# A gated mix of attention and an MLP: where the statistics' transposes, the first block's norming and the raw MLP weights stand in the opening stage

## The chip, the cores and the metric

The kernel runs on one core of one Trainium2 chip. The metric is the device time of one execution, in microseconds (us). Lower is better. TensorE (PE) multiplies matrices, VectorE (DVE) and ScalarE (ACT) empty its accumulation banks (PSUM) and do elementwise work, GpSimd (POOL) does elementwise work on on-chip tiles, and SyncE (SP) issues nearly all the DMA transfers. Each engine works through its own instructions in the order in which the program lists them.

## The reference

With S = 2048 tokens, D = 576 channels, 32 heads of 18 and F = 4608 hidden units, for one input `x`:

```
g = sigmoid((x * gate_w).sum(-1, keepdims=True))
q, k, v = split of x @ wqkv into 32 heads
a = softmax(q k^T / sqrt(18)) v, heads joined, @ wo
y = (x - mean) / sqrt(var + 1e-5)
b = gelu(y @ w1 + b1) @ w2 + b2
out = g * a + (1 - g) * b
```

Everything is float32. The kernel splits operands of the large products into a high and a low part of a faster 32-bit format and adds three products (high by high, low by high, high by low).

## The kernel before

**Two stages.** The opening stage goes through the tokens in four blocks of 512 (`tb` 0 to 3) and computes Q, K, V and the normed input of the MLP, which it parks in DRAM (`qk_scr`, `v_scr`, `y_scr`). It takes about the first 250 us. Then a loop of 512 steps weaves attention (scores, exponentials, products with V) and the MLP's matmuls, one instruction list for the whole rest. All order is written by hand: there is no scheduler behind it. What stands in a program list first runs first on its engine.

**A block** has 17 steps `g`: nine Q/K groups (`qk_group`, 14 matmuls of 512 columns, L879 to L882) and eight V groups (`v_group`, 14 matmuls of 288 columns, L900 to L903). Each group fills one of four PSUM banks (`ps_a`), and ACT (L885, L907) and DVE (L886, L911) empty it. From the group's values the high part `hh` and low part `hl` are made, and SP stores them (L888, L889, L914). Between groups stand these helpers, at steps that a table gives:

- `norm(tb, 0)` and `norm(tb, 1)`: DVE takes mean and variance of 256 tokens each (L847, L848); stage 1 ends with a square root on ACT (L854) and a chain of small DVE operations up to a reciprocal (L853 to L860). `norm(tb, 2)` and `norm(tb, 3)` form the gate's logits (L865). For block 0 alone they also norm `x` in place (L868).
- `stat_rows(tb)`: DVE copies means and reciprocals into a tile `stp` (L826, L827), PE transposes it (L829), ACT copies it out (L830) and SP stores it (L831). `load_wide(tb)` reads it back spread over all partitions into `wide` (L835). `wide` lies in the tile `qa`.
- `x_chunk(tb, c)`, c = 0 to 4: PE transposes 128 channels of `x` (L758), DVE subtracts the mean (L773, for blocks 1 to 3), ACT and DVE make high and low part (L775, L776), POOL multiplies by the reciprocal (L783). `y_parts`, `lag` steps later, makes the normed chunk's `hh` and `hl` (L798, L799), and SP stores them (L790, L792).
- `y_chunk(0, c)`: the same for block 0, from the `x` that `norm(0, 2)` and `norm(0, 3)` have normed in place: transposes (L758), L806, L807, store.
- `split_w` halves the QKV weights, seven portions during block 0 (L752, L753); `load_x(tb)` loads the next tokens into one of two buffers `x`.
- Rounds of scores (`next_round`): four matmuls (L227) and four maxima on DVE (L229), from block 1 on. They use four more PSUM banks.

`BLOCK[tb]` holds the steps of block `tb` at which the helpers for block `tb + 1` stand: `stats` (stages 0 and 1 at this step and the next), `rows`, `wide`, `gate` (stages 2 and 3), `x` (the first of five chunks), `lag`, `load`. `N_AT` does it for block 0's own norming. Within one step the group comes first, then the norming of block 0, then the helpers of the next block, then rounds.

**The MLP's generator** `mlp()` is stepped by hand in the opening stage: its first step issues the loads of raw weights (`load_w1`, L371; `load_w2`, L377) into the two buffers `x`, its second sets up the loads of the normed high part of block 0 (`high`, copied by ACT at L631). `defer(n, fn)` runs `fn` at the n-th `run_due` from now; the opening stage calls `run_due` as `SLOTS` tells.

Of the kernel before, what the change touches and what calls it, by code (L numbers as in the profile page):

```python
# [8 lines left out]
F32 = mybir.dt.float32  # L9
# [7 lines left out]
P = 128  # L17
# [7 lines left out]
TB = 512  # L25
# [29 lines left out]
          lambda g: 2 * (g in (4, 5, 6, 7, 8, 10, 12, 14))]  # L55
SLOTS = [lambda g: 0, lambda g: 0, lambda g: int(g >= 4), lambda g: 1 if g < 9 else 2]
SKIP = 0
N_AT = 5
BLOCK = [dict(stats=3, rows=5, wide=7, gate=9, x=12, lag=3, load=13),
         dict(stats=0, rows=2, wide=3, gate=3, x=5, lag=2, load=0),  # L60
         dict(stats=0, rows=2, wide=3, gate=3, x=5, lag=2)]
W_AT = {0: 1, 1: 2, 2: 3, 4: 4, 6: 5, 7: 6}
W_CUT = (0, 128, 416, 704, 992, 2 * D, 3 * D - 288, 3 * D)
NSTEP = 512
# [4 lines left out]
def gated_mix_kernel(ctx: ExitStack, tc: tile.TileContext, x, wqkv, wo, w1, b1, w2, b2, gate_w, out):  # L69
    nc = tc.nc  # L70
    x = x[0]
# [20 lines left out]
    gate = const.tile([P, NT], F32, name="gate")  # L92
# [8 lines left out]
    pp = ctx.enter_context(tc.tile_pool(name="pp", bufs=2))  # L101
# [41 lines left out]
    def defer(n, fn):  # L143
        later.append((slot[0] + n, fn))
# [191 lines left out]
    def mlp():  # L336
# [26 lines left out]
        def load_w1(q):  # L363

            if (1, q) in LOADED or q >= NQ0:
                return
            LOADED[1, q] = slot[0] + LAND
            fc = chunk(q)[2]
            for h in range(2):
                src = w1[:, (fc + h) * P:(fc + h + 1) * P]  # L370
                nc.sync.dma_start(raw1(q)[64 * h:64 * h + 64], src.rearrange("(c p) n -> p c n", p=64))  # L371

        def load_w2(c):
            if (2, c) in LOADED or c >= NFC:
                return
            LOADED[2, c] = slot[0] + LAND
            nc.sync.dma_start(raw2(c), w2[c * P:(c + 1) * P, :])  # L377
# [241 lines left out]
                HT.pop((i, j))  # L619
                W2.pop((i * (G // 2) + j // 2, j % 2))  # L620

        for q in range(2):
            load_w1(q)
            for c in range(2 * q, 2 * q + 2):
                load_w2(c)
        yield 1
        Y[0] = big_tile()

        def high(c):
            dma_r(nc.sync, Y[0][0:64, c:c + 3, :], y_scr[0, 0, c:c + 3].rearrange("c p n -> p c n"))  # L630
            defer(6, lambda: nc.scalar.activation(Y[0][64:128, c:c + 3, :], Y[0][0:64, c:c + 3, :], AF.Copy))  # L631
        for c in range(0, 9, 3):
            defer(1 + 2 * c // 3, lambda c=c: high(c))
        yield 1
        prep(0)
        prep_w2(0)
# [16 lines left out]
        for i in range(n + 1):  # L653
            q = 2 * i
# [14 lines left out]
    stream = [mlp()]  # L669
# [36 lines left out]
    with ExitStack() as a:  # L706
# [127 lines left out]
            rows = bcast_rows(st_scr[tb], 8 * P)  # L834
            nc.sync.dma_start(wide, rows.rearrange("p (a n) -> p a n", a=2))  # L835

        rstds = {}

        def norm(tb, stage):

            xv = x_view(tb)
            ts_ = slice(4 * tb, 4 * tb + 4)
            if stage < 2:
                for t in (2 * stage, 2 * stage + 1):
                    st6 = sm.tile([P, 2, nc.vector.BN_STATS_DIM], F32, name="st6")
                    for n in range(2):
                        nc.vector.bn_stats(st6[:, n, :], xv[:, t, n * ND:(n + 1) * ND])  # L847
                    nc.vector.bn_aggr(stats[:, tb * 4 + t, :], st6)  # L848
            if stage == 1:
                rstd = rstds[tb] = sm.tile([P, 4], F32, name="rstd")  # L850
                sd = sm.tile([P, 4], F32, name="sd")
                var = sm.tile([P, 4], F32, name="var")
                nc.vector.tensor_scalar(var, stats[:, ts_, 1], LN_EPS, None, op0=ALU.add)  # L853
                nc.scalar.activation(sd, var, AF.Sqrt)  # L854

                nc.vector.reciprocal(rstd, sd)
                nc.vector.tensor_mul(rstd, rstd, var)
                nc.vector.tensor_add(sd, sd, rstd)
                nc.vector.tensor_scalar(sd, sd, 0.5, None, op0=ALU.mult)
                nc.vector.reciprocal(rstd, sd)  # L860
            if stage >= 2:
                junk = pp.tile([P, 2, 2, TB], F32, name="p").rearrange("p a b c -> p (a b c)")
                for t in (2 * stage - 4, 2 * stage - 3):
                    tt = 4 * tb + t
                    nc.vector.scalar_tensor_tensor(junk[:, :D], xv[:, t, 0:D], 1.0, gwb, op0=ALU.mult, op1=ALU.mult,  # L865
                                                   accum_out=glog[:, tt:tt + 1])
                    if tb == 0:
                        nc.vector.tensor_scalar(xv[:, t, :], xv[:, t, :], stats[:, tt, 0:1], rstds[tb][:, t:t + 1],  # L868
                                                op0=ALU.subtract, op1=ALU.mult)
# [66 lines left out]
        for tb in range(NB):  # L936
            work = [(qk_group, (tb, mt)) for mt in (range(9) if tb < 2 else (4, 0, 1, 2, 3, 5, 6, 7, 8))] + [(v_group, (tb, t, n)) for t in range(4) for n in range(2)]
            for g, (fn, args) in enumerate(work):
                if tb == 0:
                    if g in W_AT:  # L940
                        n = W_AT[g]
                        split_w(n, nc.gpsimd if 2 < n < 6 else nc.vector)
                        if n + 2 < 7:
                            load_w(n + 2)
                    if g == 10:
                        nc.sync.dma_start(b2b, bcast_rows(b2, D))
                        nc.sync.dma_start(b1r, b1.rearrange("(c p) -> c p", p=P))
                if tb == NB - 1 and g == 16:
                    args += (lambda: next(stream[0]),)
                fn(*args)  # L950
                next_turn()
                if tb == 0:
                    if 0 <= g - N_AT < 4:
                        norm(0, g - N_AT)
                    if 0 <= g - 8 < 5:
                        y_chunk(0, g - 8)
                if tb + 1 < NB:
                    at = BLOCK[tb]
                    if g == at.get("load"):
                        load_x(tb + 2)  # L960
                    if g in (at["stats"], at["stats"] + 1):
                        norm(tb + 1, g - at["stats"])
                    if g == at["rows"]:
                        stat_rows(tb + 1)
                    if g == at["wide"]:
                        load_wide(tb + 1)
                    if g in (at["gate"], at["gate"] + 1):
                        norm(tb + 1, g - at["gate"] + 2)
                    c = g - at["x"]
                    if 0 <= c < 5:  # L970
                        x_chunk(tb + 1, c)
                        after(at["lag"], lambda tb=tb, c=c: y_parts(tb + 1, c))
                if tb == 2 and g == 11:
                    next(stream[0])
                if tb == NB - 1:
                    if g == 1:
                        load_k(0, 3 * TB, S)
                    if g == 2:
                        load_q(1)
                        next(stream[0])  # L980
                    if g == 9:
                        qkstack.close()
                        wp1 = mstack.enter_context(tc.tile_pool(name="m_w1", bufs=3))
                        wp2 = mstack.enter_context(tc.tile_pool(name="m_w2", bufs=4))
                        next(stream[0])

                        nc.scalar.activation(gate, glog, AF.Exp, scale=-1.0)
                    if g == 14:
                        nc.vector.tensor_scalar(gate, gate, 1.0, None, op0=ALU.add)
                        nc.vector.reciprocal(gate, gate)  # L990
                        nc.vector.tensor_scalar(gate1, gate, -1.0, 1.0, op0=ALU.mult, op1=ALU.add)
                    if g == 7:
                        ps = psum(ps_a)
                        nc.tensor.transpose(ps[:, :NFC], b1r, ident[:NFC, :NFC])
                        nc.vector.tensor_copy(b1t, ps[:, :NFC])
                if tb == 1 and g == 5:
                    load_q(0)
                    load_k(0, 0, TB)
                if tb == 1 and g == 9:
                    load_k(0, TB, 2 * TB)  # L1000
                if tb == 2 and g == 10:
                    for c0, c1 in ((0, 3), (3, 5)):
                        dma_r(nc.sync, low[0:64, c0:c1], y_scr[0, 1, c0:c1].rearrange("c p n -> p c n"))
                        defer(6, lambda c0=c0, c1=c1: nc.scalar.activation(low[64:128, c0:c1], low[0:64, c0:c1], AF.Copy))
                if tb == 2 and g == 4:
                    load_k(0, 2 * TB, 3 * TB)
                for _ in range(ROUNDS[tb](g)):
                    next_round()
                for _ in range(SLOTS[tb](g)):
                    run_due()  # L1010
# [306 lines left out]
```

## Time and profile before

| | |
|---|---|
| median of 3 runs | 2264.46 us (2262.61 to 2265.9) |
| the profiled execution | 2265.41 us, its span 2263.6 us, mean granted clock 0.995 |
| busy over the span | PE 98%, DVE 73%, ACT 63%, POOL 44% |
| bytes moved by DMA | 329.23 MB, 145 GB/s |

A row of the timeline gives start, length, engine, line, operation, output<-input, count, and in brackets how long the engine stood idle before it and what ended that. Rows of one kind that follow each other are merged (x12), and a row's length overlaps the next one's start a little, since matmuls are pipelined. A row of the windows gives for each engine the busy time in that stretch, then the granted clock of PE as a share of full speed, the DMA engines' busy share and the GB/s. A row of the waits gives the total, the number of waits and the longest.

### The profile page before, as it was taken

The page shows a single profiled execution, that of the slowest core. Times are in us where ns is not written, and L with a number is a line of the kernel's source. Part 1 is how long each engine was busy: PE and PEld are TensorE (multiplying, and loading weights), DVE is VectorE, ACT ScalarE, POOL GpSimd, SP SyncE. Part 2 cuts the span into 40 slices and gives each one's busy share as a digit, 9 for nine tenths or more (in the row PEclk, how much of TensorE's full clock was granted, in tenths as well). Part 3 has the DMA queues.
Part 4 walks back from the last instruction along what each step waited for, and adds up shares of the span by engine and source line. Part 5 has one row for each costly group of instructions (what it writes and reads, how often), then busy time and mean ns, then how long its engine had stood idle before and what let it go on. Part 6 is the DMA issues. An engine that isn't in the chain of part 4 may idle for free.

```text
span 2263.6 us, 51585 instructions
## 1 busy us (share of the span) xinstructions
PE 2224.4 (98%) x20528; PEld 1585.9 (70%) x20528; DVE 1646.2 (73%) x2886; ACT 1428.2 (63%) x2653; POOL 1002.5 (44%) x1001
## 2 busy tenths in 40 slices
PE   7999999999999999999999999999999999999999
PEld 5877766667667676676776767667676767767668
DVE  5565677777777777777777777777777777777734
ACT  3322676777776666666666666666665666666772
POOL 3311556666665444444452444444444444444710
PEclk9999999999999999999999999999999999999999
DMA  7747644445456533333254523243354323332264
GB/s 232 259 163 230 224 154 160 147 152 163 140 191 175 160 102 116 101 114 128 98 159 149 169 99 118 101 136 105 116 170 150 106 97 113 110 129 95 101 219 165
DMA packets 164104, 329.23 MB, mean 145 GB/s; under 512 B 56814, under 2 KB 84074, under 8 KB 153134
## 3 DMA queue, kind: packets, MB, share of 16 engines
q1 hardware_dynamic: 161766, 322.19, 43.8%
q8 instruction: 162, 2.65, 0.5%
q10 hardware_dynamic: 1968, 3.70, 0.4%
q14 instruction: 80, 0.66, 0.1%
q0 software_dynamic: 128, 0.03, 0.0%
HBM read 233.47 MB, written 96.17 MB: 146 GB/s over the span
## 4 chain that ended last, share of the span: by engine, by line
PE 87%; DVE 2%; ACT 1%; DMA 1%; issue 1%; POOL 1%; SPq 0%; ACTq 0%; POOLq 0%
PE ps L285 20%; PE ps L572 19%; PE ps L484 19%; PE ps L267 13%; PE ps L227 10%; PE ps L1202 3%; PE ps L879 2%; DVE m L229 1%; PE ps L900 1%; DMA x<-in_B_w_dram 1%; ACT zz L537 0%; DMA v_scr<-vt 0%; POOL w L180 0%; SPq L371 0%; ACT p L270 0%
## 5 line engine op out<-in xcount | busy, mean ns | idle before, releaser
L229 DVE TENSOR_REDUCE m<-ps 128x1 f32<-128x512 f32 x2048 | 1312.3, 685 | 413.1 <-PE ps L227 387.8
L270 ACT ACTIVATE p<-ps 128x512 f32<-128x512 f32 x1368 | 741.2, 596 | 381.1 <-PE ps L267 376.3
L484 PE MATMUL ps<-big,w 64*128 64x512 f32 x3708 | 568.2, 393 | 2.0 <-DVE vt L911 1.2
L180 POOL TENSOR_SCALAR zz<-zz 128x512 f32<-128x512 f32 x288 | 178.4, 619 | 748.6 <-ACT zz L537 733.7
L270 ACT ACTIVATE ring<-ps 128x512 f32<-128x512 f32 x680 | 369.0, 596 | 189.2 <-PE ps L267 186.8
L572 PE MATMUL ps<-w,hh 64*128 64x288 f32 x4352 | 483.6, 294 | 1.9 <-DVE x L589 0.9
L267 PE MATMUL ps<-qa,ka 56*128 56x512 f32 x2048 | 459.2, 421 | 3.2 <-ACT p L270 1.7
L572 PEld LDWEIGHTS ps<-w,hh 64*128 64x128 f32 x4352 | 423.8, 186 | 29.9 <-DVE x L589 3.3
L227 PE MATMUL ps<-ka,qa 54*128 54x512 f32 x2048 | 434.2, 398 | 0.8
L484 PEld LDWEIGHTS ps<-big,w 64*128 64x128 f32 x3708 | 368.4, 187 | 68.5 <-ACT p L270 1.4
L180 POOL TENSOR_TENSOR zz<-zz,z 128x512 f32<-128x512 f32 x288 | 371.7, 1291 | 24.0
L267 PEld LDWEIGHTS ps<-qa,ka 56*128 56x128 f32 x2048 | 213.1, 184 | 221.5 <-DVE m L229 181.1
L572 PE MATMUL ps<-w,hl 64*128 64x288 f32 x2176 | 347.6, 292 | 0.8 <-POOL hl L180 0.8
L285 PE MATMUL ps<-p,vt 128*32 128x512 f32 x2560 | 322.8, 598 | 0.0
L227 PEld LDWEIGHTS ps<-ka,qa 54*128 54x128 f32 x2048 | 218.5, 185 | 25.9 <-DVE m L229 5.5
L572 PEld LDWEIGHTS ps<-w,hl 64*128 64x128 f32 x2176 | 230.9, 185 | 1.2 <-POOL hl L180 1.1
L180 POOL TENSOR_TENSOR hl<-zz,hh 128x512 fp32r<-128x512 f32 x136 | 176.6, 1299 | 11.4
L180 POOL TENSOR_TENSOR w<-x,w 128x576 fp32r<-128x576 f32 (+1 forms) x54 | 98.6, 1843 | 179.3 <-ACT w L392 157.7
L285 PE MATMUL ps<-ring,vt 128*32 128x512 f32 x1280 | 168.7, 598 | 0.0
L285 PEld LDWEIGHTS ps<-p,vt 128*32 128x32 f32 x2560 | 67.0, 109 | 142.5 <-issue 136.3
L879 PE MATMUL ps<-big,wqk 128*128 128x512 f32 x432 | 115.7, 418 | 4.1 <-ACT v L909 3.6
L589 DVE SCALAR_TENSOR_TENSOR x<-ps,x 128x288 f32<-128x288 f32 x256 | 104.1, 448 | 8.6 <-PE ps L572 8.6
(124 smaller groups left out, 1501.2 us busy)
## 6 DMA issues: line engine op xcount, KB each, us to landing
w<-w_scr SPq DMA_DIRECT2D x54, 1152.0 KB
w<-w_scr SPq DMA_DIRECT2D x108, 576.0 KB
x<-in_B_w_dram SPq DMA_DIRECT2D x72, 288.0 KB
w_scr<-w SPq DMA_DIRECT2D x18, 1152.0 KB
w_scr<-w SPq DMA_DIRECT2D x36, 576.0 KB
qa<-qk_scr SPq DMA_DIRECT2D x192, 72.0 KB
ka<-qk_scr SPq DMA_DIRECT2D x84, 144.0 KB
qk_scr<-hh SPq DMA_DIRECT2D x36, 256.0 KB
```

The lines of the kernel that those rows point to most:

```text
L180: fn(*args, **kw)
L227: nc.tensor.matmul(ps, qa[r0:r0 + 54, t * P:(t + 1) * P], ka[r0:r0 + 54, kb * TB:(kb + 1) * TB], start=True, stop=True)
L229: nc.vector.tensor_reduce(M4[u][:, h, t, kb:kb + 1], ps, axis=AX.X, op=ALU.max)
L267: nc.tensor.matmul(ps[h], ka[r0:r0 + 56, kc * P:(kc + 1) * P], qa[r0:r0 + 56, qb * TB:(qb + 1) * TB], start=True, stop=True)
L270: nc.scalar.activation(RING[n % 3][:, qb, h], ps[h], AF.Exp, scale=SCALE)
L285: nc.tensor.matmul(OB[u][r:r + 32, :], v[:, k, 19 * h:19 * h + 32], RING[c % 3][:, qb, h, :], start=(k == 0), stop=(k == NT - 1))
L484: nc.tensor.matmul(ps[h], wt[w_][r, c, :], y[r, c, :], start=(k == 0), stop=(k == 26))
L572: mm = nc.tensor.matmul(ps[nn][:, :ND], h_[r, tok], w_[p_][r, cs[nn]], start=(k == 0), stop=(k == 6 * G - 1))
L589: nc.vector.scalar_tensor_tensor(dst, ps[nn][:, :ND], 0.5, b2b[:, cs[nn]] if g == 0 else dst, op0=ALU.mult, op1=ALU.add)
L879: nc.tensor.matmul(ps, w_[:, c, ms], big[:, s_, :], start=(k == 0), stop=False)
L900: nc.tensor.matmul(ps[:, :ND], big[:, s_, tok], w_[:, c, cs], start=(k == 0), stop=False)
L1202: nc.tensor.matmul(ps[:, :ND], OT[b][2][:, s_, tok], w_part(w_, c)[:, cs], start=(k == 0), stop=(k == 13))
```

## The change

Block 0's own norming starts at steps 3 and 4 and ends at 7 and 8 (before: 5 to 8), and its five transposed chunks move from steps 8 to 12 to steps 12 to 16, behind instead of ahead of block 1's chunks. The statistics of each following block are taken earlier relative to `stat_rows`, which now stands two or three steps after them; chunks, gate stages and token loads move with it. The two gate stages share one scratch tile. The raw MLP weights, issued in one go at step 11 of block 2, are issued from step 0 of block 3 in five portions, and the three loads of `high` come two slots later.

```
-N_AT = 5
-BLOCK = [dict(stats=3, rows=5, wide=7, gate=9, x=12, lag=3, load=13),
-         dict(stats=0, rows=2, wide=3, gate=3, x=5, lag=2, load=0),
-         dict(stats=0, rows=2, wide=3, gate=3, x=5, lag=2)]
+N_AT = {3: 0, 4: 1, 7: 2, 8: 3}
+BLOCK = [dict(stats=0, rows=4, wide=5, x=9, lag=3, gate=15, load=16),
+         dict(stats=2, rows=5, wide=6, x=7, lag=2, gate=13, load=1),
+         dict(stats=0, rows=3, wide=4, x=6, lag=2, gate=12)]
...
-        for q in range(2):
-            load_w1(q)
-            for c in range(2 * q, 2 * q + 2):
-                load_w2(c)
+        load_w1(0)
+        for late, fn, k in ((1, load_w2, 0), (1, load_w2, 1), (3, load_w1, 1), (4, load_w2, 2), (4, load_w2, 3)):
+            defer(late, lambda fn=fn, k=k: fn(k))
...
-            defer(1 + 2 * c // 3, lambda c=c: high(c))
+            defer(3 + 2 * c // 3, lambda c=c: high(c))
...
-                junk = pp.tile([P, 2, 2, TB], F32, name="p").rearrange("p a b c -> p (a b c)")
+                if stage == 2:
+                    junks[tb] = pp.tile([P, 2, 2, TB], F32, name="p").rearrange("p a b c -> p (a b c)")
+                junk = junks[tb]
...
-                    if 0 <= g - N_AT < 4:
-                        norm(0, g - N_AT)
-                    if 0 <= g - 8 < 5:
-                        y_chunk(0, g - 8)
+                    if g in N_AT:
+                        norm(0, N_AT[g])
+                    if g >= 12:
+                        y_chunk(0, g - 12)
...
-                if tb == 2 and g == 11:
-                    next(stream[0])
                 if tb == NB - 1:
+                    if g == 0:
+                        next(stream[0])
```

The edit shifts line numbers by one, so that the rows of the changed program below show, for example, L825 and L826 for the copies into `stp` that are L826 and L827 before.

On VectorE in block 0, the copies into `stp` stood before behind stage 0 of block 0's norming (two pairs of L847 and L848):

```order
L860 RECIPROCAL rstd<-sd 128x4
L886 TENSOR_TENSOR hl<-ps,hh 128x512
L847 BN_STATS st_385<-x 128x6 x2
L848 BN_AGGR stats<-st_385 128x2
L847 BN_STATS st_389<-x 128x6 x2
L848 BN_AGGR stats<-st_389 128x2
L826 COPY stp<-stats 128x4
L827 COPY stp<-rstd 128x4
```

In the changed program the same copies stand there behind stage 1 of block 0's norming, with its chain up to the reciprocal:

```order
L887 TENSOR_TENSOR hl<-ps,hh 128x512
L846 BN_STATS st_372<-x 128x6 x2
L847 BN_AGGR stats<-st_372 128x2
L846 BN_STATS st_376<-x 128x6 x2
L847 BN_AGGR stats<-st_376 128x2
L852 TENSOR_SCALAR var<-stats 128x4
L855 RECIPROCAL rstd<-sd 128x4
L856 TENSOR_TENSOR rstd<-rstd,var 128x4
L857 TENSOR_TENSOR sd<-sd,rstd 128x4
L858 TENSOR_SCALAR sd<-sd 128x4
L859 RECIPROCAL rstd<-sd 128x4
L825 COPY stp<-stats 128x4
```

So in block 0 more VectorE work stands directly ahead of the copies than before, although block 1's own reciprocals (not in these rows) are three steps back.

On TensorE at the end of block 0's Q/K groups, the first transposes of normed `x` stood between the last Q/K group (L881, L882) and the first V group (L900):

```order
L881 MATMUL ps<-big,wqk_125 128x512
L882 MATMUL ps<-big,wqk_126 128x512
L758 MATMUL ps<-ident,x 128x128 x4
L900 MATMUL ps<-wv_127,big 128x288
L900 MATMUL ps<-wv_128,big 128x288
```

In the changed program the V group follows at once, and the first transposes behind it are those of block 1's raw tokens:

```order
L882 MATMUL ps<-big,wqk_125 128x512
L883 MATMUL ps<-big,wqk_126 128x512
L901 MATMUL ps<-wv_127,big 128x288
L901 MATMUL ps<-wv_128,big 128x288
L901 MATMUL ps<-wv_127,big 128x288 x2
```

The transposes that need the normed block 0 now come three V groups later.

On SyncE's queue at the end of block 2, the raw MLP weights (L371, L377) stood ahead of the store of V (L914):

```order
L371 DMA x<-in_B_w_dram 64x9x128 x2
L377 DMA x<-in_B_w_dram 128x576 x2
L371 DMA x<-in_B_w_dram 64x9x128 x2
L377 DMA x<-in_B_w_dram 128x576 x2
L914 DMA v_scr<-vt_110 128x780
```

In the changed program they stand behind all of block 2's stores, between the Q/K stores (L889, L890) of block 3 and the reads of K and Q (L136):

```order
L371 DMA x<-in_B_w_dram 64x9x128 x2
L377 DMA x<-in_B_w_dram 128x576 x2
L889 DMA qk_scr<-hh 128x512
L890 DMA qk_scr<-hl 128x512
L136 DMA ka_107<-qk_scr 18x512 x6
L889 DMA qk_scr<-hh 128x512
L890 DMA qk_scr<-hl 128x512
L136 DMA qa_105<-qk_scr 18x1024 x6
L371 DMA x<-in_B_w_dram 64x9x128 x2
L889 DMA qk_scr<-hh 128x512
L890 DMA qk_scr<-hl 128x512
L377 DMA x<-in_B_w_dram 128x576 x2
```

From there to the end of the program, the order of the instructions on every engine is the same in both, but for one of the three copies of `high`.

More of the change, by code (lines that the diff above doesn't have):

```diff
@@ L835, in load_wide @@
             nc.sync.dma_start(wide, rows.rearrange("p (a n) -> p a n", a=2))
-        rstds = {}
+        rstds, junks = {}, {}
         def norm(tb, stage):
```

## The prediction

> **What bounds the kernel now.** I read the windows first, with one cut where the opening stage ends.
>
> ```profile
> 0.00:250.00 250.00, 222.97 (x1141) 181.07 (x1143) 148.05 (x298) 79.81 (x144) 68.37 (x59) 0.95 0.68 214
> 250.00:2180.00 1930.00, 1922.47 (x18818) 1340.72 (x18814) 1462.51 (x2524) 1316.45 (x2449) 934.14 (x942) 1.00 0.41 134
> ```
>
> The first number behind the comma is PE's busy time. In the loop PE is busy 1922 of 1930 us at full clock: nothing to gain there, and the change leaves its order alone. In the opening stage PE stands idle for 250 - 223 = 27 us, and its clock is 0.95. The loop follows the opening stage on the same engine without a break, so what PE saves before 250 us the whole kernel should save. The waits of PE in this stage name the places:
>
> ```profile
> PE ps L829 <- DVE stp L827: 11.0, 3, 4.1
> PE ps L758 <- DVE x L868: 5.7, 4, 2.3
> PE ps L879 <- ACT v L909: 3.6, 1, 3.6
> PE ps L484 <- DVE vt L911: 1.2, 1, 1.2
> ```
>
> The first three are what the change aims at: the statistics' transposes (one each in blocks 0, 1 and 2), the transposes of the normed block 0, and a stall in block 3. The fourth lies at the loop's start and stays. Each long wait is paid twice, because the clock falls behind it (third number from the end):
>
> ```profile
> 52.80:56.80 4.00, 4.00 (x18) 3.98 (x19) 0.69 (x1) 0.73 (x2) 0.00 (x0) 0.50 0.37 135
> 87.30:91.30 4.00, 4.00 (x13) 3.20 (x14) 0.00 (x0) 0.27 (x1) 0.00 (x0) 0.66 1.07 398
> 248.40:252.40 4.00, 2.84 (x24) 2.55 (x25) 2.60 (x6) 2.00 (x4) 0.00 (x0) 1.00 1.13 232
> ```
>
> Behind the four waits for L868 it is 0.50, behind block 1's wait for L827 0.66, but behind the 1.2 us at the loop's start it stays at 1.00.
>
> **Block 0, statistics.** The copies into `stp` now stand behind stage 1 of block 0's own norming. The rows for the price, PE first:
>
> ```profile
> 34.57 0.48 PE L829 MATMUL ps<-ident,stp 128*128 128x128 f32 x1 [4.09 <-DVE stp L827]
> 39.27 2.96 PE L879 MATMUL ps<-big,wqk 128*128 128x512 f32 x12
> 42.54 2.96 PE L879 MATMUL ps<-big,wqk 128*128 128x512 f32 x12
> ```
>
> and DVE:
>
> ```profile
> 19.16 1.66 DVE L753 TENSOR_TENSOR wqk<-p,wqk 128x1440 fp32r<-128x1440 f32 x1 [4.43 <-ACT wqk L752]
> 20.74 0.68 DVE L886 TENSOR_TENSOR hl<-ps,hh 128x512 fp32r<-128x512 f32 x1
> 28.49 0.81 DVE L847 BATCH_NORM_STATS2 st<-x 128x6 f32<-128x288 f32 x2
> 31.85 0.66 DVE L886 TENSOR_TENSOR hl<-ps,hh 128x512 fp32r<-128x512 f32 x1
> 32.43 0.81 DVE L847 BATCH_NORM_STATS2 st<-x 128x6 f32<-128x288 f32 x2
> 34.32 0.12 DVE L826 COPY stp<-stats 128x4 f32<-128x4 f32 x1
> ```
>
> A Q/K group takes 42.54 - 39.27 = 3.27 us. Stage 1 takes 31.85 - 28.49 = 3.36, an eviction 0.6, stage 0 takes 34.32 - 32.43 = 1.89, and from the copies to PE's transpose pass 0.25. The transpose now follows group 4, which ends at 34.57 - 4.09 - 3.27 = 27.2. DVE from group 1's eviction at 20.74: 21.35, block 1's stage 1 to 24.7, two evictions, which wait for ACT (it does a weight split behind the square root), to about 26.7, stage 0 to 28.6, group 4's eviction to 29.2, stage 1 to 32.6, transpose at 32.8. The wait is 5.6 instead of 4.1: **-1.5** (with evictions straight away 4.9, so -0.8). The slow clock behind it stays as it is. Block 1's statistics at step 0 cost nothing: their 1.89 fit into the 4.43 that DVE stands idle ahead of the split at 19.16, if block 1's tokens have landed by 17; before, they were read later than that, so the trace doesn't show when they land, and I take 0, down to -1.
>
> **Block 0, normed transposes.**
>
> ```profile
> 52.86 3.23 PE L900 MATMUL ps<-wv,big 128*128 128x288 f32 x12
> 59.73 1.84 PE L900 MATMUL ps<-wv,big 128*128 128x288 f32 x12
> 73.91 3.05 PE L879 MATMUL ps<-big,wqk 128*128 128x512 f32 x12
> 65.82 0.68 DVE L773 TENSOR_TENSOR p<-ps,qa 128x512 f32<-128x512 f32 x1
> 67.78 0.68 DVE L773 TENSOR_TENSOR p<-ps,qa 128x512 f32<-128x512 f32 x1
> ```
>
> The last Q/K group ends at 42.54 + 3.27 = 45.8, the first V group starts at 52.86. Of these 7.05 us the transposes need 0.35, so 6.7 go. The first two V groups with a transpose behind each take 59.73 - 52.86 = 6.9 at the slow clock; the other six groups, with seven transposes, take 14.2 to 73.91, 2.3 for a pair, so 2.2 more go. What becomes late next is DVE: it comes out of the norming about 2 us behind PE, a chunk takes it 67.78 - 65.82 = 1.96, and steps 12 and 13 hold two chunks. Following the four banks through, PE waits about 0.9 at steps 13 and 14. **+8.0**, between +6 and +9.
>
> **Block 1.**
>
> ```profile
> 87.28 0.30 PE L829 MATMUL ps<-ident,stp 128*128 128x128 f32 x1 [3.06 <-DVE stp L827]
> 87.33 4.41 PE L879 MATMUL ps<-big,wqk 128*128 128x512 f32 x12
> 136.21 0.39 PE L882 MATMUL ps<-big,wqk 128*128 128x512 f32 x1
> 137.27 0.69 DVE L886 TENSOR_TENSOR hl<-ps,hh 128x512 fp32r<-128x512 f32 x1 [0.68 <-ACT hh L885]
> 143.60 0.68 DVE L886 TENSOR_TENSOR hl<-ps,hh 128x512 fp32r<-128x512 f32 x1
> 144.58 0.45 PE L829 MATMUL ps<-ident,stp 128*128 128x128 f32 x1 [3.85 <-DVE stp L827]
> 144.68 5.47 PE L879 MATMUL ps<-big,wqk 128*128 128x512 f32 x12
> ```
>
> The wait does not vanish. The copies still stand behind the eviction of the group just ahead of the transpose: 136.60 to 137.27 until DVE starts on it, 144.58 - 143.60 = 0.98 from there to the transpose, so 1.65. That saves 3.06 - 1.65 = 1.4, and the first matmuls behind it lose 4.41 - 2.96 = 1.45 less, if 1.65 leaves the clock alone as 1.2 does. Against it, `wide` and the chunks come late:
>
> ```profile
> 100.73 2.17 SPq L136 DMA_DIRECT2D qa<-qk_scr  x6
> 102.95 2.72 SPq L136 DMA_DIRECT2D ka<-qk_scr  x6
> 115.87 2.48 DVE L229 TENSOR_REDUCE m<-ps 128x1 f32<-128x512 f32 x4
> 117.29 1.61 PE L227 MATMUL ps<-ka,qa 54*128 54x512 f32 x4
> 150.56 0.73 PE L227 MATMUL ps<-ka,qa 54*128 54x512 f32 x4
> ```
>
> and from the groups by shape, where the number behind the comma is the mean in ns:
>
> ```profile
> L911 DVE COPY vt<-ps 128x288 f32<-128x288 f32 x16 | 7.2, 453 | 14.0 <-DMA v_scr<-vt 9.3 <-PE ps L903 4.7
> L865 DVE SCALAR_TENSOR_TENSOR p<-x,gwb 128x576 f32<-128x576 f32 x16 | 12.0, 752 | 0.2
> ```
>
> The read of `wide` (L835) now stands behind the twelve issues of L136 (2.17 + 2.72 = 4.9 us of SP), and one step nearer to the first chunk: 1 to 3 us late by my walk through the queues. And the chunks, at steps 7 to 11, meet the rounds of steps 9 and 11, among V groups of 2 us. From the first chunk to the block's end DVE has 25 us (five chunks of 1.96, four rounds of 2.4, four copies of 0.4, two gate stages of 1.6, one eviction), PE 23 (the same steps at 3.3, 2.0, 0.35 and 0.66 a piece). With `wide` 2 us late, DVE ends 4 us behind; the free banks take about 1.2 of it, and for the rest the rounds find their banks full: about -2.8, between -0.5 (`wide` in time) and -4 (3 us late). In return the 1.61 - 0.73 = 0.9 of the old place go. Sum **+1.0**.
>
> **Block 2.** The wait goes from 3.85 to 1.65, +2.2, and the slow clock with it, 5.47 - 2.96 = +2.5. Chunks stand one step later, between Q/K groups mostly, where DVE and PE are even (29 us against 31); of one old stall, 2.07 in the next row where 0.73 is usual, I take half, +0.7:
>
> ```profile
> 178.06 2.07 PE L227 MATMUL ps<-ka,qa 54*128 54x512 f32 x4
> ```
>
> **+5.4.**
>
> **Block 3.** The place is PE's wait for ACT and, on the chain, what ACT waited for:
>
> ```profile
> 201.40 4.53 PE L879 MATMUL ps<-big,wqk 128*128 128x512 f32 x12 [3.58 <-ACT v L909]
> 191.72 9.03 DMA v_scr<-vt
> ```
>
> The last row is a V store that needed 9.03 us because the raw weights stood ahead of it; ACT waited for the V buffer it frees, and PE for ACT. With the weights behind the V stores the 3.6 go, and 4.53 - 2.96 = 1.6 of slow clock: **+5.1**. The weights are wanted at step 9, nine groups of 3.27 or some 30 us after their first issue, by splits whose order is unchanged. What could be late is K's last quarter, read behind the first two portions; its first use is three groups later, so I take 0, down to -3.
>
> **The sum.** -1.5 + 8.0 + 1.0 + 5.4 + 5.1 = 18.0 us. The profiled execution took 2265.41 (its span is 2263.6), 0.95 above the median of the runs; from the median, 2264.46 - 18.0 = 2246.5.
>
> [...]
>
> **The rivals.**
>
> *Short waits throttle too.* Four waits of at most 2.3 us brought 0.50, so the two of 1.65 may. Against it: they stand alone, between full groups, like the 1.2 that left 1.00. The 1.45 and 2.5 stay: 2246.5 + 3.95 = 2250.5. Chance 0.15.
>
> *Block 2's tokens come late.* Their load moves from step 13 to 16 of block 0, behind the last stores, about 7 us later against PE. Statistics at step 2 of block 1 leave about 1.6 us of slack by my walk. If they land 3 us beyond it, block 1's wait grows to 4.6 and keeps its slow clock: 2246.5 + 3 + 1.45 = 2251. Chance 0.12.
>
> *The buffers of `hh` close a circle: slower.* In steps 12 to 16 of block 0, eleven buffers of `hh` are asked of a ring of six within 11 us. Each must be stored before reuse; SP's stores stand behind V stores that wait for DVE, DVE behind the ACT copy, ACT for the buffer. One turn is about 4.2 us by my walk (stores of a chunk issued behind the V store, landed, then L806, L807, L911). I find one turn, absorbed by the banks. From the fourth on it eats the whole gain; with five, one per chunk, and the clock lost once (2.2) the time is 2246.5 + 21 + 2.2 = 2269.7. For it: nothing in the trace drains so many buffers. Against it: the DMA engines were busy 0.37 in the row at 52.8. Chance 0.07.
>
> *The loop gives it back.* If the weights' splits at the loop's start are late by what the opening stage gained, PE waits at L484 instead, and the time stays at 2264. Their order behind PE's groups speaks against it. Chance 0.05.
>
> **How the numbers follow.** The forecast has 0.61; a gain over 22 is part of it. Under 0.2%, or 4.5 us, a measurement of this kernel can't be told from no change. Faster: 0.61 + 0.15 + 0.12 = 0.88; same 0.05; slower 0.07. The forecast's own range is 2242 (no new stall in blocks 0 and 1) to 2253 (every bound at its worse end but the rivals'). To hold 8 in 10 it takes in the first two rivals and part of their sum: 2241.5 to 2256.
>
> **What would show it.** Right: waits for L827 of about 5.6, 1.65 and 1.65; no wait for L868; none for L909; clock 0.5 to 0.7 once, behind block 0's statistics; the loop's first L484 18 us earlier. Wrong: PE waits in block 1's V groups of over 4 us, a wait for BN statistics on a DMA at block 1's third group, an L806 row behind a store, or an L484 that waits for weights.

## The result and the profile after

The changed kernel takes 2257.85 us (median of 9 runs, 2256.74 to 2260.52) against 2264.46 before (9 runs here too): ratio 0.9974, 95% interval 0.9964 to 0.9984. It is faster by 6.6 us where 18 were predicted; the time lies outside the range. The profiled execution took 2257.29, its span 2255.4.

The window of the changed kernel's opening stage:

```profile
0.00:242.00 242.00, 218.93 (x1141) 177.94 (x1143) 149.87 (x298) 79.18 (x144) 69.35 (x59) 0.96 0.69 220
```

The opening stage still holds 242 - 219 = 23 us of idle PE (27 before), and its clock only rose from 0.95 to 0.96. The waits of PE in it:

```profile
PE ps L828 <- DVE stp L826: 9.1, 3, 5.7
PE ps L757 <- DVE big L775: 5.9, 1, 5.9
PE ps L757 <- DMA x<-in_A_x_dram: 5.0, 1, 5.0
PE ps L484 <- ACT p L270: 1.1, 1, 1.1
PE ps L901 <- DVE big L775: 0.8, 1, 0.8
```

The waits for L868 and for L909 are gone, as forecast. The second row is new: 5.9 us in one piece, PE's transposes of raw tokens waiting for a bank. (The third, for the first tokens, was 4.8 before.) Where each block's Q/K groups (from L880) and V groups (from L901) begin on PE places it:

| us | before | after | gain | predicted |
|---|---|---|---|---|
| block 0, Q/K and V | 43.63 + 21.05 | 38.50 + 20.31 | +5.9 | +6.5 |
| block 1 | 36.33 + 19.68 | 32.36 + 30.03 | -6.4 | +1.0 |
| block 2 | 41.11 + 20.11 | 35.99 + 21.66 | +3.6 | +5.4 |
| block 3, to the loop's first L484 | 58.56 | 53.72 | +4.8 | +5.1 |
| the rest of the span | 2013.9 | 2013.6 | +0.3 | 0 |

Blocks 0 and 3 came out close, block 2 fell 1.8 short, and block 1 lost 6.4 where it should have won 1.0. The timeline of the changed kernel around the statistics' transposes (L828), PE:

```profile
32.84 0.45 PE L828 MATMUL ps<-ident,stp 128*128 128x128 f32 x1 [5.75 <-DVE stp L826]
32.94 4.72 PE L880 MATMUL ps<-big,wqk 128*128 128x512 f32 x12
89.69 0.33 PE L828 MATMUL ps<-ident,stp 128*128 128x128 f32 x1 [1.76 <-DVE stp L826]
89.77 3.04 PE L880 MATMUL ps<-big,wqk 128*128 128x512 f32 x12
146.17 0.33 PE L828 MATMUL ps<-ident,stp 128*128 128x128 f32 x1 [1.62 <-DVE stp L826]
```

The waits are 5.75, 1.76 and 1.62 for a forecast of 5.6, 1.65 and 1.65, and the clock falls only behind the first (twelve matmuls in 4.72 us there, in 3.04 and 3.06 behind the other two). So block 1's loss isn't at its transpose; it follows among the chunks of `x`. PE:

```profile
96.38 0.60 PE L757 MATMUL ps<-ident,x 128*128 128x128 f32 x4
108.41 1.09 PE L757 MATMUL ps<-ident,x 128*128 128x128 f32 x4 [5.86 <-DVE big L775]
...
110.58 3.25 PE L901 MATMUL ps<-wv,big 128*128 128x288 f32 x12
```

DVE, at its first subtraction of the mean:

```profile
106.21 0.69 DVE L772 TENSOR_TENSOR p<-ps,qa 128x512 f32<-128x512 f32 x1 [8.26 <-DMA qa<-st_scr]
```

and SP's queue, from the store of the statistics (L830) to the read of `wide` (L834):

```profile
92.06 0.28 SPq L830 DMA_DIRECT2D st_scr<-strow  x1
92.78 4.28 SPq L136 DMA_DIRECT2D qa<-qk_scr  x6
97.44 2.42 SPq L136 DMA_DIRECT2D ka<-qk_scr  x6
100.83 0.43 SPq L834 DMA_DIRECT2D qa<-st_scr  x1
```

Read upwards: PE stands because the banks are full, the banks because DVE stands 8.26 us at the first subtraction, DVE because `wide` lands only at 106.1, and it lands then because its read leaves SP at 100.83. In the course of the wait the clock falls, at 104.9, and it stays at half until 115.1 (third number from the end):

```profile
100.00:108.00 8.00, 2.55 (x20) 2.22 (x17) 1.12 (x2) 1.06 (x2) 0.96 (x1) 0.81 0.71 206
108.00:116.00 8.00, 7.59 (x34) 6.63 (x35) 6.67 (x12) 2.65 (x7) 5.33 (x5) 0.55 0.28 95
```

The five merged rows from 108.41 to 116.8 take 3.0 more than the same rows at full clock. 5.86 + 3.0 = 8.9 of the 10.35 that the V half of block 1 grew by.

### The profile page after: what moved, and what is told of

Read it like the earlier page. It is cut to its first block, busy times and chain, and to the rows that moved or that the text cites. A ratio compares the mean times of both kernels' runs of the same rounds, so it can differ in the third digit from the quotient of the medians.

```text
span 2255.4 us, 51587 instructions
## 1 busy us (share of the span) xinstructions
PE 2220.2 (98%) x20528; PEld 1582.7 (70%) x20528; DVE 1648.1 (73%) x2886; ACT 1428.6 (63%) x2653; POOL 1003.6 (44%) x1001
## 4 chain that ended last, share of the span: by engine, by line
PE 91%; DVE 4%; DMA 2%; ACT 1%; issue 1%; POOL 1%; SPq 0%; ACTq 0%; POOLq 0%; DVEq 0%
PE ps L285 20%; PE ps L484 19%; PE ps L572 19%; PE ps L267 13%; PE ps L227 10%; PE ps L880 3%; PE ps L1203 3%; DVE m L229 1%; PE ps L901 1%; DMA x<-in_B_w_dram 1%; ACT zz L537 0%; POOL w L180 0%; PE ps L757 0%; DMA qk_scr<-hh 0%; ACT p L270 0%
## 5 line engine op out<-in xcount | busy, mean ns | idle before, releaser
L484 PE MATMUL ps<-big,w 64*128 64x512 f32 x3708 | 567.9, 393 | 1.9 <-ACT p L270 1.1
L484 PEld LDWEIGHTS ps<-big,w 64*128 64x128 f32 x3708 | 368.2, 186 | 68.5 <-ACT p L270 1.4
L880 PE MATMUL ps<-big,wqk 128*128 128x512 f32 x432 | 110.4, 403 | 0.4 <-DVE wqk L752 0.4
```

The lines of the kernel that those rows point to most:

```text
L484: nc.tensor.matmul(ps[h], wt[w_][r, c, :], y[r, c, :], start=(k == 0), stop=(k == 26))
L880: nc.tensor.matmul(ps, w_[:, c, ms], big[:, s_, :], start=(k == 0), stop=False)
```

## The experiments

Theory 1: the gain that is missing went into `wide` of block 1. Its read is late, PE runs out of banks, and the clock falls behind that. Theory 2, the rivals: short waits lower the clock too; or the tokens' late load is the cause; or the moved table alone does it, whatever the queues hold. Gains below are against the kernel before on the same chip (2264.49 for the first four, 2263.4 for the last four).

**The weights alone** (with the later loads of `high`), on the kernel before:

```
-        for q in range(2):
-            load_w1(q)
...
+        load_w1(0)
+        for late, fn, k in ((1, load_w2, 0), (1, load_w2, 1), (3, load_w1, 1), (4, load_w2, 2), (4, load_w2, 3)):
+            defer(late, lambda fn=fn, k=k: fn(k))
...
-                if tb == 2 and g == 11:
-                    next(stream[0])
...
+                    if g == 0:
+                        next(stream[0])
```

> The kernel before with the five portions of raw weights (and the later loads of the normed high part) alone. If block 3's stall was the weights standing ahead of the V store, as both theories have it: no wait of PE behind the V copies at block 3's third group (3.6 before), no slow clock there (1.6), so 5 us less than the kernel before, about 2259.4. If the weights bring a wait of their own at the loop's start, less than 3 us are gained.

Measured 2261.54 (2260.55 to 2263.37), ratio 0.9986 (0.9978 to 0.9995): 2.95 us where 5 were expected. Block 3 takes 53.73, 4.8 less, as in the changed kernel: that step is shown. But the loop is 2.1 longer than before in the profiled execution. Its first row of L484 on PE:

```profile
243.18 1.36 PE L484 MATMUL ps<-big,w 64*128 64x512 f32 x6 [1.12 <-ACT p L270]
```

The same row in the changed kernel, behind a wait of the same length, keeps the full clock:

```profile
241.84 0.97 PE L484 MATMUL ps<-big,w 64*128 64x512 f32 x6 [1.12 <-ACT p L270]
```

So the clock falls behind a wait of 1.12 us in one kernel and not in the other; the last section comes back to that.

**The read of `wide` ahead of the twelve issues of L136** (the changed kernel, the issues one step later):

```
-                if tb == 1 and g == 5:
+                if tb == 1 and g == 6:
```

> The changed kernel with the twelve issues that read Q and K in block 1 one step later, so that the read of the spread statistics (wide) is issued ahead of them. Theory 1, the order of SyncE's queue: wide is issued at about 93.5 instead of 100.8 and has landed by 99, so the wait of 5.9 us at block 1's third chunk goes, and its slow clock (about 3 us); the rounds at step 9 may wait 1 to 3 us for Q and K instead. About 5 us less than the changed kernel, 2253. Theory 2, the DMA engines are full whatever the order: wide is issued early but lands at 101 or later, PE still waits over 2 us, and less than 3 us are gained.

Measured 2256.73 (2253.47 to 2257.73), ratio 0.9964 (0.9951 to 0.9976): 7.8 us. SP, and DVE's first subtraction:

```profile
92.37 0.28 SPq L830 DMA_DIRECT2D st_scr<-strow  x1
97.06 0.32 SPq L834 DMA_DIRECT2D qa<-st_scr  x1
```

```profile
101.97 0.69 DVE L772 TENSOR_TENSOR p<-ps,qa 128x512 f32<-128x512 f32 x1 [2.89 <-DMA qa<-st_scr]
```

`wide` comes 4.2 us earlier, PE's wait for a bank shrinks from 5.86 to 0.49, and block 1 takes 56.2 instead of 62.4: 6.2 of the 7.4 us by which the prediction missed there. That is theory 1 in the profile, though not at its times: the read leaves at 97.06 where 93.5 was expected, and DVE can start at 101.97, not at 99. The profiled execution was the fastest of the five (its span is 3.7 under that of the changed kernel), the median only 1.1 lower, which is theory 2's "less than 3 us"; so the time alone doesn't show it, and what the slower executions lost, and where, is not on record.

**The tokens' load later** (1152 KB by the profile, not 1.3 MB), out of the way of block 0's stores:

```
-         dict(stats=2, rows=5, wide=6, x=7, lag=2, gate=13, load=1),
+         dict(stats=2, rows=5, wide=6, x=7, lag=2, gate=13, load=9),
```

> The changed kernel with the last block's tokens (1.3 MB) loaded at step 9 of block 1 instead of step 1. Theory 1, the order of SyncE's queue: wide is still issued behind the twelve issues, at 99 or later, and the wait at block 1's third chunk is still 4 us or more; at most 2 us are gained. Theory 2, the DMA engines are full: with 4 us of transfers out of the way the twelve issues go through in about 5 us, wide lands at about 101 instead of 106, the wait shrinks to 1 us or less without slow clock, and about 7 us are gained, 2251.

Measured 2255.21 (2254.25 to 2257.95), ratio 0.9962 (0.995 to 0.9974): 9.3 us. SP:

```profile
90.29 2.92 SPq L136 DMA_DIRECT2D qa<-qk_scr  x6
93.25 2.11 SPq L136 DMA_DIRECT2D ka<-qk_scr  x6
96.33 0.43 SPq L834 DMA_DIRECT2D qa<-st_scr  x1
```

The twelve issues take 5.0 instead of 6.7: they had been slow because the load at 82.37 came on top of block 0's stores (DMA share 0.95 to 1.09 from 68 to 92 in the changed kernel). The read leaves 4.5 earlier, DVE's wait falls to 3.17, PE's to 0.77: as theory 2 has it, and without a change of the order. Either edit alone, this or the one before, brings `wide` nearly in time. Block 1 takes 60.6 all the same, since here the clock fell twice: behind its transpose, after a wait of 1.81, and among the rounds of the V half, after 1.11. PE's first row behind the transpose, and the windows of the two slow stretches:

```profile
89.38 4.53 PE L880 MATMUL ps<-big,wqk 128*128 128x512 f32 x12
```

```profile
90.54:93.92 3.38, 3.38 (x10) 2.59 (x9) 0.00 (x0) 0.00 (x0) 0.00 (x0) 0.50 0.78 207
117.85:124.64 6.79, 6.69 (x25) 5.91 (x25) 6.51 (x15) 0.00 (x0) 0.92 (x1) 0.50 0.60 228
```

**Block 0's transpose two steps later**, to take its 5.75 away:

```
-BLOCK = [dict(stats=0, rows=4, wide=5, x=9, lag=3, gate=15, load=16),
+BLOCK = [dict(stats=0, rows=6, wide=7, x=9, lag=3, gate=15, load=16),
```

> The changed kernel with block 0's statistics transposed at step 6 instead of 4 (and wide read at step 7): two steps behind block 0's own reciprocals. By both theories the wait of 5.75 us becomes one of about 1.65 as in blocks 1 and 2, without the slow clock behind it (1.8 us): 5.8 us less in block 0. If the rest moves with it, 2252; if block 1's wait is set by a backlog that starts from fixed times of the loads, part of the 5.8 is given back there.

Measured 2256.66 (2254.61 to 2259.14), ratio 0.9965 (0.9952 to 0.9979): 7.8 us. The wait in block 0 is 3.20 where 1.65 was expected, the clock falls behind it, and the block gets only 1.0 shorter (57.8 for 58.8). In block 1 the clock falls behind a wait of 2.29:

```profile
38.23 0.33 PE L828 MATMUL ps<-ident,stp 128*128 128x128 f32 x1 [3.20 <-DVE stp L826]
38.31 4.59 PE L880 MATMUL ps<-big,wqk 128*128 128x512 f32 x12
88.91 0.33 PE L828 MATMUL ps<-ident,stp 128*128 128x128 f32 x1 [2.29 <-DVE stp L826]
```

The 3.20 are no backlog of DVE's: it stood idle for 2.31 until ACT had copied the group ahead out, and then its first copy into `stp`, 0.14 in the changed kernel, took 1.74. It ended at 38.10, and a part of the weights' split on POOL at 38.08 (DVE, then POOL):

```profile
36.36 1.74 DVE L825 COPY stp<-stats 128x4 f32<-128x4 f32 x1
```

```profile
34.86 3.22 POOL L752 TENSOR_TENSOR wv<-p,wv 128x1440 fp32r<-128x1440 f32 x1 [4.34 <-ACT wv L751]
```

Whether the one held up the other no run here shows.

**The transpose one step behind its copies**, in all blocks (transpose, copy and store stand behind the next step's group):

```
+            after(1, lambda: stat_store(tb))
+
+        def stat_store(tb):
```

> The changed kernel with the copies into stp where they are, but the transpose on TensorE, the copy out and the store one step later, so that a whole group of matmuls lies between copies and transpose. If PE's waits for the statistics are the distance of copy and transpose and nothing else: 5.75 becomes 2.5, 1.76 and 1.62 go, 6.6 us less, about 2251, and 2 to 4 us less again in executions where the short waits lowered the clock. The wait at block 1's third chunk stays, as wide is still read behind the twelve issues. If the clock falls for other reasons than PE's waits, nothing beyond the 6.6 is seen.

Measured 2255.67 (2254.0 to 2256.15), ratio 0.9963 (0.9951 to 0.9976): 7.7 us. PE's waits for `stp` fall from 9.1 in all to 1.3, and 1.5 us go in block 0 and 1.8 in block 2. (In block 0 the Q/K half gains 4.9, but the V half loses 3.4, with a new wait of 2.17 for a bank and a slow stretch behind it.) Block 1 keeps its 62.2, because what its transpose no longer waits comes back at the chunks (L833 is the store here, L837 the read):

```profile
98.37 0.29 SPq L833 DMA_DIRECT2D st_scr<-strow  x1
101.00 0.32 SPq L837 DMA_DIRECT2D qa<-st_scr  x1
```

```profile
107.51 1.09 PE L757 MATMUL ps<-ident,x 128*128 128x128 f32 x4 [8.58 <-DVE big L775]
```

The store now falls behind the twelve issues, and PE's wait for a bank grows to 8.58. A wait moved from one place of a chain to another: a sign that the end of the chain, `wide`, sets the time here.

**The gate stages earlier**, away from the rounds at the ends of blocks 1 and 2:

```
-         dict(stats=2, rows=5, wide=6, x=7, lag=2, gate=13, load=1),
-         dict(stats=0, rows=3, wide=4, x=6, lag=2, gate=12)]
+         dict(stats=2, rows=5, wide=6, x=7, lag=2, gate=5, load=1),
+         dict(stats=0, rows=3, wide=4, x=6, lag=2, gate=4)]
```

> The changed kernel with the gate stages of block 1 at step 5 and of block 2 at step 4, among Q/K groups instead of V groups. If VectorE is what the rounds among V groups wait for: block 2's three long rounds (0.98, 1.51 and 2.13 against 0.73) fall to 0.73, 2.4 us less, and block 1's (1.24 and 1.49) by about 1: some 3 us less, 2255. If the rounds wait for something else, nothing changes.

Measured 2256.24 (2253.8 to 2258.14), ratio 0.9969 (0.9958 to 0.998): 7.2 us. In the changed kernel the last round of block 2 (PE, then DVE) waits for maxima that stand behind the gate's products, which begin here:

```profile
184.10 2.13 PE L227 MATMUL ps<-ka,qa 54*128 54x512 f32 x4
```

```profile
180.12 0.76 DVE L866 SCALAR_TENSOR_TENSOR p<-x,gwb 128x576 f32<-128x576 f32 x1
183.21 2.48 DVE L229 TENSOR_REDUCE m<-ps 128x1 f32<-128x512 f32 x4
```

With the gates earlier the last round is back at the usual 0.73, and block 2 takes 56.25 instead of 57.65. The round before it keeps its length (1.52, and 1.51 in the changed kernel), so of the 2.4 us that were expected in block 2 the gates account for 1.4:

```profile
177.52 1.52 PE L227 MATMUL ps<-ka,qa 54*128 54x512 f32 x4
182.88 0.73 PE L227 MATMUL ps<-ka,qa 54*128 54x512 f32 x4
```

**Block 1's row of the table alone**, on the kernel before:

```
-         dict(stats=0, rows=2, wide=3, gate=3, x=5, lag=2, load=0),
+         dict(stats=2, rows=5, wide=6, x=7, lag=2, gate=13, load=0),
```

> The kernel before with block 1's new steps alone (statistics 2, rows 5, wide 6, chunks from 7, gate 13), tokens loaded early as before. Theory 1, the order of SyncE's queue is enough: wide is issued 10 us or more behind the transpose of the statistics and PE waits 4 us or more at the third chunk; block 1 gets longer than 56 us in spite of the shorter wait for the statistics, 2266 to 2268. Theory 2, it needs the bunched transfers of block 0 too: wide lands in time or 2 us late, PE waits under 1 us there, block 1 gains 1 to 3 us, 2262 to 2264.

Measured 2267.32 (2264.92 to 2268.41), ratio 1.0016 (1.0008 to 1.0025): slower. With block 0 as before, the DMA engines are less full (share 0.75 from 68 to 76, 0.86 from 76 to 84), and the issues take 4.6 again, but `wide` is late all the same (L831 is the store here, L835 the read, L758 PE's transposes):

```profile
96.51 0.29 SPq L831 DMA_DIRECT2D st_scr<-strow  x1
96.84 2.09 SPq L136 DMA_DIRECT2D qa<-qk_scr  x6
98.98 2.53 SPq L136 DMA_DIRECT2D ka<-qk_scr  x6
102.81 0.43 SPq L835 DMA_DIRECT2D qa<-st_scr  x1
```

```profile
110.55 0.63 PE L758 MATMUL ps<-ident,x 128*128 128x128 f32 x4 [1.83 <-DVE big L776]
```

PE's wait is 1.83 (DVE's 4.23), between what the two theories expected; the clock stays at 1.00, and block 1 takes 57.5, 1.5 more than before. So the new steps cost block 1 time by themselves, and the slow issues and the slow clock add the rest. The 3.9 us in the medians are more than the profiled spans show (2264.3 against 2263.6); where the other 3 are stays open.

**All together**: the split, block 0's transpose at step 5, the issues of L136 one step later, the load at step 9, the gates at 5 and 4:

```
+BLOCK = [dict(stats=0, rows=5, wide=6, x=9, lag=3, gate=15, load=16),
+         dict(stats=2, rows=5, wide=6, x=7, lag=2, gate=5, load=9),
+         dict(stats=0, rows=3, wide=4, x=6, lag=2, gate=4)]
...
+            after(1, lambda: stat_store(tb))
+
+        def stat_store(tb):
...
+                if tb == 1 and g == 6:
```

> A version from the findings: the changed kernel with the transposes one step behind the copies, block 0's copies at step 5, the twelve issues behind the read of wide, the last block's tokens at step 9 of block 1, and the gate stages of blocks 1 and 2 among Q/K groups. If waits for the statistics, the late read of wide and VectorE among V groups are the three losses, each goes: 5.75 + 1.8 slow clock in block 0, 1.7 and 1.6 in blocks 1 and 2, 5.9 + 2.3 at the third chunk, 3 at the rounds: 20 us in the opening stage less 2 for what is left of wide's lateness, and 2240 in all. If they share time (one hides another), 2245 to 2250.

Measured 2247.46 (2243.6 to 2248.09), ratio 0.9926 (0.9914 to 0.9939): 15.9 us, faster than both kernels, and in the range that was expected if the losses share time. The blocks take 57.6, 55.4, 54.4 and 53.7. The way of the statistics, unhindered now, from PE over SP to DVE and PE (L831 the transpose, L833 the store, L837 the read):

```profile
89.73 0.27 PE L831 MATMUL ps<-ident,stp 128*128 128x128 f32 x1
```

```profile
91.75 0.30 SPq L833 DMA_DIRECT2D st_scr<-strow  x1
94.51 0.34 SPq L837 DMA_DIRECT2D qa<-st_scr  x1
```

```profile
98.90 0.69 DVE L772 TENSOR_TENSOR p<-ps,qa 128x512 f32<-128x512 f32 x1 [4.21 <-DMA qa<-st_scr]
```

```profile
101.09 0.63 PE L757 MATMUL ps<-ident,x 128*128 128x128 f32 x4 [1.80 <-DVE big L775]
```

With nothing ahead of it in SP's queue, the way still takes 98.90 - 89.73 = 9.2 us, and PE waits 1.80 for it. The loop starts at 230.3, where the forecast had put it at 231.7, but here the clock fell behind the 1.12 us, and the loop is 2.1 longer than in the changed kernel.

## Why the prediction was wrong, step by step

*Block 0, statistics and normed transposes* (+6.5): right. The wait is 5.75 for 5.6, the Q/K half gave 5.1 for 5.2, the stall among the V groups is 0.83 at one place for 0.9. The V half gave 0.7 for 1.3.

*Block 1* (+1.0): this step failed. Its first half was right: the shorter wait gave 1.3 where 1.4 was counted, the kept clock 1.4 where 1.45 was. (The Q/K half got 4.0 shorter also because two more of the five chunks now stand in the V half.) The term that was mis-sized is "`wide` 1 to 3 us late", priced at -2.8 with -4 as its worse end. It was 8.26 late, by DVE's wait for it, and the V half lost 10.35. For the lateness that it assumed the price was about right: with the read ahead of the twelve issues DVE waited 2.89, and block 1 took 0.2 more than before, where 2.85 - 4 + 0.9 = -0.25 follows from the prediction's figures for 3 us.

The working took SP's twelve issues at the 4.9 us they had before; how it got from there to 1 to 3 us isn't written down. Three things made it more. First, the way of the statistics as a whole: before, the read left 6.0 us behind the store and had landed 4.9 later at most, and the first chunk came 11.5 us behind the transpose; now it comes 96.38 - 89.69 = 6.7 behind it, and the shortest way that any run showed is 9.2. Rows of before told this:

```profile
89.36 0.29 SPq L831 DMA_DIRECT2D st_scr<-strow  x1
95.40 0.54 SPq L835 DMA_DIRECT2D qa<-st_scr  x1
98.76 0.60 PE L758 MATMUL ps<-ident,x 128*128 128x128 f32 x4
```

Second, the read now stands behind the twelve issues, and these took 6.7, since the later load of tokens comes on top of block 0's later stores just then (5.0 without that load); with issues of 4.6, in the kernel with block 1's row alone, DVE still waited 4.23. Third, with a wait of 5.86 the clock falls, 3.0 more. What the free banks cover is 2.4 us, where the prediction put 1.2: DVE's wait less PE's is 2.89 - 0.49, 3.17 - 0.77, 4.21 - 1.80 and 8.26 - 5.86. In these four each us beyond cost PE one, and in the changed kernel the slow clock's 3.0 came on top.

*Block 2* (+5.4): 3.6. The wait and the clock came back as worked out (the Q/K half gave 5.1 for 4.7). The V half lost 1.55 instead of gaining 0.7: "DVE and PE are even" was worked out over the chunks and missed the last round, whose maxima stand behind the gate's products. With earlier gates the block took 56.25, a gain of 5.0.

*Block 3* (+5.1): right, 4.8 in each kernel that has the change.

*The rivals.* Short waits that throttle: not in the profiled execution of the changed kernel, but in variants of it at these very places, in block 1 (1.81, 2.15, 2.29), in block 2 (1.61, 1.62) and at the loop's start. That both waits left the clock alone in this one profile was partly luck, as the last section shows. Block 2's tokens did land late: DVE waited 2.90 us for them, and that used up the slack, with little to spare for PE. With the tokens loaded early (block 1's row alone) PE's wait for the statistics was 1.61; in the changed kernel it was 1.76, and in the variants it grew with DVE's wait for the tokens: 1.81 for 2.95, 2.15 for 3.28, 2.29 for 3.44. The circle of `hh` buffers turned once, as worked out, and cost nothing:

```profile
68.92 0.60 ACT L805 ACTIVATE hh<-ps 128x512 fp32r<-128x512 f32 x1 [1.31 <-DMA y_scr<-hh]
```

The loop gave nothing back in the changed kernel. Of the four signs of being wrong three came: PE's wait of over 4 us among block 1's V groups, DVE's wait for block 2's tokens, and the row of L805 (L806 before) behind a store.

The sum misses by 18 - 7.9 = 10.1 in the profiled span's opening stage, of which 7.4 are block 1 and 1.8 block 2. That block 1 takes 56.2 as soon as the read of `wide` leaves ahead of the twelve issues shows where most of it went. The 15.9 us of the last kernel are no repair of the forecast alone, since the split takes waits away that the change leaves in.

## What to carry to other kernels

When two steps of a table move closer together, add up everything that runs between them, the store, the wait for it, the read back and its landing, and hold that against the new distance before pricing the waits that the move removes. Here the buffers in between covered 2.4 us of lateness, and every us beyond was PE's. Ask what else the same edit puts into the queue that the step goes through: here a later load of tokens, on top of later stores, made the same twelve issues slower by a third (6.7 us for 5.0). When a wait that is removed in one place reappears further down the same chain, mend the chain's end first.

## What the runs showed that was not expected

The granted clock doesn't depend on the length of the wait alone. Behind about 1.1 us at the loop's start it fell in three profiles (first six matmuls of L484 in 1.36, 1.65 and 1.55 us) and held in the changed kernel's and four more (0.96 or 0.97). Behind the transpose of block 1 it held after 1.76 and 1.96 and fell after 1.81, 2.15 and 2.29; behind that of block 2, after 1.61 or 1.62, it fell in two profiles and held in three. Each such fall cost 1.5 to 2.1 us.

The traces keep when the granted clock changes. Up to the loop's start it is at half in the kernel before from 33.99, 51.06, 88.61, 143.22 and 201.24 us on, for 3.41, 6.83, 3.41, 6.83 and 3.41 us, and in the changed kernel from 29.81 and 104.90 on, for 6.83 and 10.24. In these two profiles each length, and each distance between two beginnings, is a whole multiple of 3.41 us to within 0.01.

So where a wait lies in time may count beside its length. That is an estimate, from the changed kernel's two beginnings and stretches of 3.41 us counted on from them: its 1.62 and 1.12, which held, are then each split over two stretches (1.31 + 0.31 and 0.72 + 0.40). Two of the waits behind which the clock fell lay whole in the 3.41 us ahead of the fall: the 1.12 of the kernel with the weights alone, from 242.06 to 243.18, with the fall at about 243.6 (clock 0.88 from 236 to 246, 0.95 from 246 to 256), and the 1.81 of the kernel with the later tokens, from 87.49 to 89.30, with the fall at about 90.5. But the 1.76 of the changed kernel, by the same count, lay whole in one stretch too, from 87.84 to 91.25, and held. What decides among these was not settled.

Single improvements of one or two us drown in such falls: the five variants of the changed kernel that alter one thing have ratios of 0.9962 to 0.9969, and none can be told from the changed kernel by its interval, all the less as the changed kernel was not run again beside them.
